# Sliding-window attention with sinks and a SwiGLU block: how the second group's keys and queries are loaded and transposed

## The chip, the cores and the metric

The kernel runs on one core of a Trainium2 chip. The metric is the device time of one execution in microseconds (us). TensorE multiplies matrices and transposes them against an identity, VectorE and ScalarE work elementwise and move results out of PSUM, GpSimd here mostly issues DMAs, and SyncE (SP) and ScalarE issue a few more.

## The reference

Cut to what matters: attention of 4 batches, 8 heads, 768 tokens, head width 64, where a query sees the 128 tokens up to its own and the first 4 tokens (the sinks); then a feed-forward block on the 3072 tokens.

```python
scores = scale * np.matmul(q, k.transpose(0, 1, 3, 2))
keep = is_sink | in_window              # first 4 keys, or 0 <= q - k < 128
a = softmax(np.where(keep, scores, -1e9))
x = np.matmul(a, v)                     # heads side by side: [3072, 512]
g = x @ w_gate                          # 512 -> 1536
out = ((g * sigmoid(g)) * (x @ w_val)) @ w_out
```

Inputs and output are float32 in DRAM; the kernel computes in bfloat16 and accumulates in float32.

## The kernel before

**Groups and blocks.** Attention goes by groups of 256 tokens, three to a batch, twelve in all (g = 0 to 11). The feed-forward block goes by blocks of tokens (SIZES, line 42: 256, 256, 256, 512, ...). The instruction order of every engine is written out by hand: `weave` runs over the feed-forward units (a gate unit is eight or four matmuls with `wg` and as many with `wv`, line 564; a down unit is twelve with `wo`, line 657) and puts attention steps of later groups between them. A program runs in that order on each engine; engines wait for each other, and for DMAs, by semaphores.

**Keys and queries.** The scores need keys and queries turned: head width on the partitions (two heads of 64 above each other), tokens along the row. The tiles `kT` and `qT` of a batch hold this for four pairs of heads. Four ways lead there:
- Group 0: `x0` and `st`, two tokens to a row, turned by `pair_T` (line 746).
- Group 1: `load_rows` (line 97) brings the tile `rows`, `step_T` (line 252) turns it. In `rows` a partition holds four successive tokens of one head (4 x 64 elements, 1 KB in DRAM, 512 B as bfloat16); partitions 0 to 63 belong to the even heads, 64 to 127 to the odd ones. Each 64x64 block is turned alone in a quarter of the array, 16 matmuls to a PSUM tile `pt` (two pairs of heads, all 256 tokens), and the copy out of PSUM puts the tokens back in order with a stride.
- Groups 2 and 3: `load_nat` (line 106) brings the tile `nat`, `step_TN` (line 273) turns it. In `nat` a partition is one token, with its eight heads side by side (each head's 64 elements are a piece of their own, 128 B as bfloat16). A 128x128 block (128 tokens, a pair of heads) is one transpose; four of them fill a bfloat16 PSUM tile `pn` (128 tokens, all heads).
- Groups 4 to 11: `nat` again, turned by DMA transposes on SP's queue.

All loads that convert float32 to bfloat16 are issued by GpSimd, in program order: `x0`, the keys and queries of group 1, the values of groups 0 and 1 (`va`, `load_v`, line 151), the first chunk of gate and value weights (`wg`, `wv`, `load_gate`, line 162); then, between a few small GpSimd computations (`kss`, `vsb`, for the sinks), two more weight chunks, the `nat` of group 2, and so on. `rows` and the `nat` of groups below 4 share a ring of three buffers (`rowp`) with the two `st` tiles.

**The work around the change on TensorE.** After group 0's scores come the transposes of group 1, then group 0's products with the values (line 494, tile `o`), the scores of group 1 (line 326, tile `s`) in three portions between them, the sink scores (line 432, `pk`), and the transposes of group 0's result (line 543, `px`), which give `xT`, the input of the first gate matmul (line 564, `pg`). The products of group 1 follow within the first gate units.

```python
    step_T(1, 0, 0, "a")
    step_T(1, 0, 1, "a")
    step_T(1, 1, 0, "v")
    step_T(1, 1, 1, "a")
    step_PV(0, 0, 0)
    step_PV(0, 0, 1)
    flush()
    step_S(1, 0)
```

`"a"` and `"v"` name the engine, ScalarE or VectorE, that copies the PSUM tile out.

Of the kernel before, what the change touches and what calls it, by code (L numbers as in the profile page):

```python
# [7 lines left out]
FP32 = mybir.dt.float32  # L8
BF16 = mybir.dt.bfloat16
# [5 lines left out]
def kernel(  # L15
# [12 lines left out]
    nc = tc.nc  # L28
    P = 128
    B, H, S, D = q.shape  # L30
# [8 lines left out]
    NP2 = H // 2  # L39
    GC = S // 256  # L40
# [14 lines left out]
    def pool(name, bufs, psum=False):  # L55
        if psum:
            return ctx.enter_context(
                tc.tile_pool(name=name, bufs=bufs, space=bass.MemoryType.PSUM))
        return ctx.enter_context(tc.tile_pool(name=name, bufs=bufs))
# [3 lines left out]
    rowp = pool("rowp", 3)  # L63
# [16 lines left out]
    def bank(shape, dtype, name):  # L80
        return psum.tile(shape, dtype, tag="b", name=name)


    rows, nats, vas = {}, {}, {}

    def by_rows(src, b, w, pairs, t0):

        hs = slice(2 * pairs.start + w, 2 * pairs.stop, 2)
        return src[b, hs, t0:t0 + 256].rearrange("p (m r) d -> m p (r d)", r=4)

    ALL = slice(0, NP2)

    def new_rows(g):
        rows[g] = rowp.tile([P, 2, NP2, 4 * D], BF16, tag="rows", name="rows")
        return rows[g]

    def load_rows(g, i):
        b, c = divmod(g, GC)
        if g not in rows:
            new_rows(g)  # L100
        for w in range(2):
            nc.gpsimd.dma_start(
                rows[g][64 * w:64 * (w + 1), i],
                by_rows((k, q)[i], b, w, ALL, c * 256))

    def load_nat(g):
        b, c = divmod(g, GC)
        x = (natp if g > 3 else rowp).tile(
            [P, 2, 2, DM], BF16, tag="nat" if g > 3 else "rows", name="nat")
        for i, src in ((0, k), (1, q)):  # L110
            for j in range(2):
                t0 = c * 256 + j * P
                nc.gpsimd.dma_start(  # L113
                    x[:, i, j].rearrange("p (h d) -> p h d", d=D),
                    src[b, :, t0:t0 + P].rearrange("h p d -> p h d"))
        nats[g] = x
# [26 lines left out]
    def load_v(g):  # L143
        if g in QG:
            return load_vm(g)
        b, c = divmod(g, GC)
        va = vpool.tile([P, 2, H, VS], BF16, tag=f"va{g}", name="va")
        nc.vector.memset(va[:, :, :, D:D + 1], 1.0)
        for j in range(2):
            t0 = c * 256 + j * P  # L150
            nc.gpsimd.dma_start(  # L151
                va[:, j, :, 0:D], v[b, :, t0:t0 + P].rearrange("h p d -> p h d"))
        vas[g] = va
# [19 lines left out]
    ident = const.tile([P, P], BF16)  # L173
# [41 lines left out]
    for i in range(2):  # L215
# [2 lines left out]
                   allow_small_or_imprecise_dtypes=True)  # L218
    nc.gpsimd.iota(tk, [[0, 1]], base=0, channel_multiplier=1,
                   allow_small_or_imprecise_dtypes=True)  # L220
    load_rows(1, 0)
    load_rows(1, 1)
    load_v(0)
    load_v(1)
    load_gate(0)
# [5 lines left out]
    kTs, qTs, es_t, e_t, xns, xTs = {}, {}, {}, {}, {}, {}  # L231
# [15 lines left out]
    def new_T(b):  # L247
        if b not in kTs:
            kTs[b] = kqtp.tile([P, NP2, S], BF16, tag="kT", name="kT")
            qTs[b] = kqtp.tile([P, NP2, S], BF16, tag="qT", name="qT")  # L250

    def step_T(g, i, p2, evict=None):
        b, c = divmod(g, GC)
        new_T(b)
        x = rows[g]
        pt = bank([P, 2, 256], FP32, "pt")
        for pp in range(2):
            p = 2 * p2 + pp
            for r in range(4):
                for w in range(2):  # L260
                    h = slice(64 * w, 64 * (w + 1))
                    nc.tensor.matmul(
                        pt[h, pp, 64 * r:64 * (r + 1)], x[h, i, p, r * D:(r + 1) * D],
                        ident[h, h], start=True, stop=True, skip_group_check=True)
        dst = (kTs, qTs)[i][b][:, 2 * p2:2 * p2 + 2, c * 256:(c + 1) * 256].rearrange(
            "q a (m r) -> q a m r", r=4)
        pt = pt.rearrange("q a (r m) -> q a m r", r=4)
        if (evict or ("a", "v")[i]) == "a":
            nc.scalar.copy(out=dst, in_=pt)
        else:  # L270
            nc.vector.tensor_copy(out=dst, in_=pt)

    def step_TN(g, i, j, evict="av"):

        b, c = divmod(g, GC)
        new_T(b)
        pt = bank([P, NP2, P], BF16, "pn")
        for p in range(NP2):
            nc.tensor.transpose(pt[:, p], nats[g][:, i, j, p * P:(p + 1) * P], ident)  # L279
        t0 = c * 256 + j * P  # L280
        dst = (kTs, qTs)[i][b][:, :, t0:t0 + P]
        if evict[i] == "a":
            nc.scalar.copy(out=dst, in_=pt)
        else:
            nc.vector.tensor_copy(out=dst, in_=pt)
# [531 lines left out]
    load_sinks(vcl, 1, B)  # L817
    build_maskq()

    step_T(1, 0, 0, "a")  # L820
    step_T(1, 0, 1, "a")
    step_T(1, 1, 0, "v")
    step_T(1, 1, 1, "a")
    step_PV(0, 0, 0)
    step_PV(0, 0, 1)
    flush()
# [98 lines left out]
```

## Time and profile before

| what | value |
|---|---|
| time, median of three runs | 233.85 us (233.03 to 235.38) |
| time of the profiled execution | 233.03 us |
| its span, first to last instruction | 231.2 us |
| TensorE matmuls, busy | 226.0 us, 98% of the span |
| VectorE, ScalarE, GpSimd, busy | 151.1, 106.3, 84.8 us |
| DMA packets | 112008, of which 99056 under 512 B |
| the transposes of group 1 (L262) | 64 matmuls, 9.45 to 11.09 us |
| first gate matmul (L564) starts | 15.09 us |

Times in the profile count from the start of the span. The 1.8 us between the span and the profiled execution's time lie around the span. "L262" is line 262; `pt<-ident,rows` is the tile written and the tiles read; "x64" is a number of instructions. PE is TensorE, PEld its weight loads, DVE VectorE, ACT ScalarE, POOL GpSimd, SP SyncE. An arrow in brackets names who ended an engine's idle time. A matmul's own length holds its way through the array, so matmuls that follow each other overlap in the listing; their pitch, start to start, is what a stream of them costs.

### The profile page before, as it was taken

Reading aid. Unit: us, or ns where it says so; the run is one execution under the profiler, and the core shown is the slowest. Engines: PE = TensorE matmul, PEld = TensorE weight load, DVE = VectorE, ACT = ScalarE, POOL = GpSimd, SP = SyncE. Lnnn points to the kernel's source line nnn. Section 1 sums busy time; section 2 is a strip of 40 time slices with the busy share of each in tenths; the row PEclk is TensorE's granted clock in tenths of the full one; section 3 lists DMA queues with packets and bytes.
Section 4 is the critical chain, followed back from the end, with each engine's and each line's share of the span. In section 5 each row is a group of like instructions: output and inputs, shape, how many; then the busy total and the mean of one; then the engine's idle time right before and its main releaser. Section 6 shows DMA issues by size and latency. Waiting matters only on the chain.

```text
span 231.2 us, 5467 instructions
## 1 busy us (share of the span) xinstructions
PE 226.0 (98%) x2171; PEld 126.8 (55%) x2171; DVE 151.1 (65%) x327; ACT 106.3 (46%) x212; POOL 84.8 (37%) x123
## 2 busy tenths in 40 slices
PE   7989999999999999999999999999999999999994
PEld 3669545786556854455454454454454544487443
DVE  5898888767650797960897960697960599778000
ACT  4784496367523827323626412735512823333221
POOL 8997965960500906904526064362000000000000
PEclk9999999999999999999999999999999999999999
DMA  7999999999998998998999999989814102000132
GB/s 134 164 188 178 179 199 206 163 155 125 154 168 211 80 132 103 145 197 124 134 124 118 147 87 203 144 107 131 94 48 136 48 0 45 3 0 0 69 116 91
DMA packets 112008, 28.04 MB, mean 121 GB/s; under 512 B 99056, under 2 KB 109040, under 8 KB 111984
## 3 DMA queue, kind: packets, MB, share of 16 engines
q0 software_dynamic: 79904, 14.29, 80.7%
q1 hardware_dynamic: 30672, 11.58, 28.5%
q10 hardware_dynamic: 1408, 1.84, 2.8%
q8 instruction: 17, 0.28, 0.5%
q14 instruction: 7, 0.06, 0.1%
HBM read 29.13 MB, written 6.29 MB: 153 GB/s over the span
## 4 chain that ended last, share of the span: by engine, by line
PE 93%; DMA 4%; DVE 1%; ACTq 0%; ACT 0%; issue 0%
PE pg L564 27%; PE pv L564 27%; PE pd L657 27%; PE o L494 3%; PE s L382 3%; DMA wg<-in_moe_w_gate_dram 3%; DMA st<-in_q_dram 2%; PE o L463 1%; PE pn L279 1%; PE o L454 1%; PE pk L432 1%; PE s L326 0%; PE px L543 0%; DVE kT L755 0%; PE pt L746 0%; PE s L765 0%
## 5 line engine op out<-in xcount | busy, mean ns | idle before, releaser
L592 DVE SCALAR_TENSOR_TENSOR u<-th,pg 128x512 bf16<-128x512 f32 x72 | 49.1, 683 | 45.3 <-ACT th L584 44.9
L564 PE MATMUL pg<-xT,wg 128*128 128x512 bf16 (+1 forms) x368 | 74.2, 333 | 0.5 <-DMA wg<-in_moe_w_gate_dram 0.5
L564 PE MATMUL pv<-xT,wv 128*128 128x512 bf16 (+1 forms) x368 | 74.1, 333 | 0.0
L584 ACT ACTIVATE th<-pg 128x512 f32<-128x512 f32 x72 | 43.8, 608 | 59.4 <-PE pg L564 59.2
L657 PE MATMUL pd<-wo,ht 128*128 128x512 bf16 (+2 forms) x300 | 65.9, 370 | 0.0
L564 PEld LDWEIGHTS <-wg 128*128 128x128 bf16 x368 | 35.2, 98 | 26.5 <-DMA wg<-in_moe_w_gate_dram 0.7
L564 PEld LDWEIGHTS <-wv 128*128 128x128 bf16 x368 | 34.6, 98 | 22.8 <-issue 0.2
L607 DVE TENSOR_TENSOR ht<-u,pv 128x512 bf16<-128x512 bf16 x60 | 41.2, 686 | 4.5 <-PE pv L564 0.4
L657 PEld LDWEIGHTS <-ht 128*128 128x128 bf16 x300 | 27.6, 98 | 28.4
L662 ACT ACTIVATE ot<-pd 128x512 f32<-128x512 f32 (+1 forms) x24 | 14.3, 595 | 50.2 <-PE pd L657 50.2
L395 ACT ACTIVATE e<-s 128x512 bf16<-128x512 f32 x54 | 28.5, 614 | 5.8 <-PE s L382 5.4
L113 POOL DMA_DIRECT2D nat<-in_k_dram x20 | 17.8, 896 | 28.6 <-DMA qT<-nat 27.1
L511 DVE TENSOR_TENSOR xn<-o,rcp 128x256 bf16<-128x256 f32 x45 | 17.9, 420 | 0.7
L128 POOL DMA_DIRECT2D vm<-in_v_dram x24 | 17.8, 772 | 1.1 <-DMA va<-in_v_dram 0.8
L113 POOL DMA_DIRECT2D nat<-in_q_dram x20 | 17.8, 908 | 1.0 <-DMA wg<-in_moe_w_gate_dram 0.8
L494 PEld LDWEIGHTS <-e 128*128 128x128 bf16 x256 | 11.5, 98 | 6.0 <-issue 0.2
L404 DVE TENSOR_TENSOR e<-e,maskq 128x768 bf16<-128x768 bf16 x24 | 13.1, 552 | 1.9 <-ACT e L395 1.9
L151 POOL DMA_DIRECT2D va<-in_v_dram x12 | 10.7, 921 | 4.5 <-DMA wo<-in_moe_w_out_dram 2.5
L703 POOL CAST warmed<-xT 1x1 f32<-1x1 bf16 x3 | 0.5, 175 | 28.5 <-DMA xT<-xn 28.5
L503 DVE RECIPROCAL rcp<-o 128x4 f32<-128x4 f32 x48 | 7.1, 171 | 4.8 <-PE o L494 4.5
L664 DVE TENSOR_SCALAR ot<-pd 128x128 f32<-128x128 f32 x1 | 0.3, 292 | 14.3 <-PE pd L657 14.3
L333 ACT ACTIVATE e<-s 128x512 bf16<-128x512 f32 x16 | 8.3, 625 | 0.3 <-PE s L326 0.3
(86 smaller groups left out, 141.4 us busy)
## 6 DMA issues: line engine op xcount, KB each, us to landing
out_dram<-ot SPq DMA_DIRECT2D x17, 256.0 KB
nat<-in_k_dram POOLq DMA_DIRECT2D x20, 128.0 KB, 4.2
nat<-in_q_dram POOLq DMA_DIRECT2D x20, 128.0 KB, 5.2
va<-in_v_dram POOLq DMA_DIRECT2D x12, 128.0 KB, 5.5
wg<-in_moe_w_gate_dram POOLq DMA_DIRECT2D x6, 256.0 KB, 7.1
wv<-in_moe_w_val_dram POOLq DMA_DIRECT2D x6, 256.0 KB, 7.6
wo<-in_moe_w_out_dram POOLq DMA_DIRECT2D x4, 384.0 KB, 11.1
out_dram<-ot ACTq DMA_DIRECT2D x6, 256.0 KB
```

What stands on the lines that cost most here:

```text
L113: nc.gpsimd.dma_start(x[:, i, j].rearrange("p (h d) -> p h d", d=D), src[b, :, t0:t0 + P].rearrange("h p d -> p h d"))
L128: nc.gpsimd.dma_start(vms[b][p0:p1, t - 1, :, 0:D], v[b, :, t0:t0 + p1 - p0].rearrange("h p d -> p h d"))
L395: nc.scalar.activation(e_t[g][:, e0:e0 + 512], pss[g][w, i], AF.Exp, scale=scale)
L404: nc.vector.tensor_tensor(e, e, m.broadcast_to([P, 2, 384]), op=ALU.mult)
L494: nc.tensor.matmul(o, l, r, start=(c == 0 and i == 0), stop=(i == len(mms) - 1), skip_group_check=True)
L511: nc.vector.tensor_tensor(xn, po[:, :, 0:D], rcp.broadcast_to([P, 4, D]), op=ALU.mult)
L564: nc.tensor.matmul(ps[:, i * n:(i + 1) * n], ws[fi][:, c, fo * P:(fo + 1) * P], xTs[tb][:, c], start=(c == 0), stop=(c == DMC - 1))
L584: nc.scalar.activation(th, pg, AF.Tanh, scale=0.5)
L592: nc.vector.scalar_tensor_tensor(u, th, 1.0, pg, op0=ALU.add, op1=ALU.mult)
L607: nc.vector.tensor_tensor(hts[tb][:, f:f + 512 // SIZES[tb]].rearrange("p a n -> p (a n)"), u, pv, op=ALU.mult)
L657: nc.tensor.matmul(po, hts[tb][:, f, ts * P:(ts + 1) * P], wos[f // n][:, f % n, lo:hi], start=(f == 0), stop=(f == DFC - 1))
L662: nc.scalar.activation(ot, po, AF.Copy, scale=0.5)
```

## The change

Group 1 takes the way of groups 2 and 3: `load_rows(1, 0)` and `load_rows(1, 1)` become `load_nat(1)` at the same place in GpSimd's order (again four DMAs of 128 KB each, as written), and the four calls of `step_T` become four calls of `step_TN` at the same place in TensorE's order. The copies out of PSUM stay on the same engines: ScalarE, ScalarE, VectorE, ScalarE. `load_rows`, `by_rows`, `new_rows` and `step_T` are removed. The ring `rowp` has the same tiles in the same order, one `nat` in place of one `rows`.

```diff
-    load_rows(1, 0)
-    load_rows(1, 1)
+    load_nat(1)
     load_v(0)
     load_v(1)
     load_gate(0)
...
-    step_T(1, 0, 0, "a")
-    step_T(1, 0, 1, "a")
-    step_T(1, 1, 0, "v")
-    step_T(1, 1, 1, "a")
+    step_TN(1, 0, 0, "aa")
+    step_TN(1, 0, 1, "aa")
+    step_TN(1, 1, 0, "av")
+    step_TN(1, 1, 1, "aa")
     step_PV(0, 0, 0)
```

The first argument after the group says keys (0) or queries (1). For `step_T` the next one is a half of the heads, for `step_TN` it is a half of the group's 256 tokens.

More of the change, by code (lines that the diff above doesn't have):

```diff
@@ L81, in bank @@
         return psum.tile(shape, dtype, tag="b", name=name)
[L84 to L104, printed above, removed]
+    nats, vas = {}, {}
     def load_nat(g):
@@ L250, in new_T @@
             qTs[b] = kqtp.tile([P, NP2, S], BF16, tag="qT", name="qT")
[L252 to L271, printed above, removed]
     def step_TN(g, i, j, evict="av"):
```

## Prediction

> **What bounds the kernel now.** I read the page first, for the engine that is always busy and for what ends its idle time.
>
> ```profile
> span 231.2 us, 5467 instructions
> PE 226.0 (98%) x2171; PEld 126.8 (55%) x2171; DVE 151.1 (65%) x327; ACT 106.3 (46%) x212; POOL 84.8 (37%) x123
> ...
> L564 PE MATMUL pg<-xT,wg 128*128 128x512 bf16 (+1 forms) x368 | 74.2, 333 | 0.5 <-DMA wg<-in_moe_w_gate_dram 0.5
> L564 PE MATMUL pv<-xT,wv 128*128 128x512 bf16 (+1 forms) x368 | 74.1, 333 | 0.0
> ```
>
> TensorE is busy for 226.0 of 231.2 us, and the feed-forward matmuls of L564 wait once in the whole run: 0.5 us, for the first gate weights. Second, TensorE's timeline around that wait and around the transposes that change:
>
> ```profile
> 9.45 1.64 PE L262 MATMUL pt<-ident,rows 64*64 64x64 bf16 x64
> 11.02 0.42 PE L494 MATMUL o<-va,e 128*128 128x65 bf16 x8
> 11.73 0.62 PE L326 MATMUL s<-qT,kT 64*128 64x128 bf16 x12 [0.29 <-DVE qT L271]
> 12.28 0.66 PE L494 MATMUL o<-va,e 128*128 128x65 bf16 x16
> ...
> 14.09 0.55 PE L326 MATMUL s<-qT,kT 64*128 64x128 bf16 x6
> 15.09 1.05 PE L564 MATMUL pg<-xT,wg 128*128 128x256 bf16 x8 [0.45 <-DMA wg<-in_moe_w_gate_dram]
> 16.07 0.29 PE L454 MATMUL o<-vsb,es 32*128 32x260 bf16 x4
> ...
> 24.75 0.61 PE L279 MATMUL pn<-ident,nat 128*128 128x128 bf16 x8
> ```
>
> TensorE is ready at 14.64 and starts the gate at 15.09, when the weights land. The chain of waits holds nothing but TensorE from there to the stores at the end. So the end is 15.09 plus a fixed run of matmuls: **what moves the first gate matmul moves the end one for one**, and what moves TensorE's readiness by less than 0.45 moves nothing. Third, what the weights wait for, in GpSimd's timeline, where all these loads are issued one behind the other:
>
> ```profile
> 3.23 1.28 POOL L102 DMA_DIRECT2D rows<-in_k_dram  x2
> 4.47 1.27 POOL L102 DMA_DIRECT2D rows<-in_q_dram  x2
> 5.67 3.60 POOL L151 DMA_DIRECT2D va<-in_v_dram  x4
> 9.17 0.85 POOL L162 DMA_DIRECT2D wg<-in_moe_w_gate_dram  x1
> ...
> 14.56 1.13 POOL L304 TENSOR_TENSOR vsb<-vcf,diag_h 128x260 bf16<-128x260 f32 x1
> 15.65 1.84 POOL L113 DMA_DIRECT2D nat<-in_k_dram  x2
> 17.46 1.78 POOL L113 DMA_DIRECT2D nat<-in_q_dram  x2
> ```
>
> GpSimd issues without a pause from 1.24 to 10.8, and the first wg (issued at 9.17, landed 5.87 later) stands behind the four loads that the change replaces. Fourth, the DMA view in two stretches of one microsecond, 10 to 11 (only va packets, of 128 B) and 16 to 17 (only weight packets, of 512 B):
>
> ```profile
> DMA packets 1196, 0.15 MB, mean 151 GB/s; under 512 B 1196, under 2 KB 1196, under 8 KB 1196
> ```
>
> ```profile
> DMA packets 398, 0.20 MB, mean 196 GB/s; under 512 B 16, under 2 KB 398, under 8 KB 398
> ```
>
> The same bytes take longer in short packets, and the engines work without a break from 6 us on, so extra service time is passed down the queue.
>
> **The change part by part.** *Loads.* Removed: four rows DMAs (64 partitions x 4 pairs = 256 packets of 512 B each, issued 0.61 apart: 3.23 to 5.67 is 2.44 for four). Added: four nat DMAs (128 partitions x 8 heads = 1024 packets of 128 B, the same bytes; the nat of group 2 is issued in the same form from 15.65 to 19.19, the va from 5.67 to 9.17, both 0.875 to 0.885 apart). Two prices follow.
> - By issue: 4 x (0.875 - 0.61) = 1.06 us later for everything behind it on GpSimd.
> - By service: 1024 packets at 1146 to 1196 in a microsecond are 0.86 to 0.89 us; 256 of 512 B take 0.67 at the 382 of that size seen in 16 to 17, and 0.77 at the 333 of the busier 7 to 8. Four times the difference is 0.35 to 0.9 us.
>
> Which of the two sets the landing? The va wait in a line today (first issued at 5.67, while their packets begin only near 8.8, as the rows end), so part of the later issue is taken up by that line, and service counts. But with 0.875 per issue and 0.88 per service the line hardly shrinks any more. I take **+0.75 for the landing of the first wg** (nearer to the service price), 0.35 to 1.06 as its ends: 15.05 becomes 15.8.
>
> *Transposes.* Removed: 64 quarter matmuls, 9.45 to 11.09. Added: 16 full ones. The 128-column matmuls of the first groups (pt of L746) follow each other by 0.106 us; the nat transposes of L279, later, by 0.056 (8 in 0.61, of which 0.22 is the last one's own length). TensorE runs at half rate until about 10.56 (below), so ten transposes go at 0.106 and the rest at 0.056: done at 10.9, if the data are there. The fourth load is issued at 3.23 + 3 x 0.875 = 5.86 and lands, at the 4.7 of the va, at 10.55; its four transposes then end at 10.95. Against 11.09: **nothing gained, nothing lost** on TensorE. That the instructions are four times fewer is worth nothing, because two quarters run at a time and a quarter has half the columns.
>
> *Evictions.* Four as before, three on ScalarE and one on VectorE. ScalarE's cost 0.53 each (L283, two in 1.07) for 0.54 (L269); VectorE's 0.42 (L285) for 0.70 (L271). But a tile now holds 128 tokens of all heads instead of all tokens of four heads, so the first scores of group 1 need all four evictions, where they needed one of each today. ScalarE is free of exponentials at 10.42, and three evictions end at 12.0: the scores start at 12.05 for 11.73, 0.3 later. The va that feed the products before and between land 0.75 later, 11.25 and 12.1 for the first two, and are used at 11.3 and 12.6: inside the same 0.3. TensorE and the copies of xT are then ready at 14.95 for 14.64. **The later wg (15.8) hides this**; without that cover, with wg at today's 15.05, 14.95 would still be in time.
>
> *What else is queued on GpSimd.* The sink keys (kss), the vsb product and the following weights and nat move with it. wv lands 16.45 today and is wanted at 16.79, the second wg 17.77 for 18.15, the k half of group 2 24.25 for 24.75: all are passed on by the same 0.75 as TensorE's own delay, so the margins of 0.3 to 0.5 stay. The thinnest is vsb: done at 15.69, wanted at 16.07; by issue it moves 1.06 and TensorE 0.75, which leaves 0.07. SP's and ScalarE's DMA queues are not touched: SP issues nothing from 5.2 to 40 us. From 57 us on GpSimd waits for what TensorE paces, and DMA has pauses.
>
> **Sum:** +0.75 for wg, 0 for transposes, 0 for evictions. Profiled execution: 233.03 + 0.75 = 233.8. That execution is the fastest of the three; on their median of 233.85 it is **234.6 us**, 0.3% slower, and inside the 1% that a measurement of this kernel can about tell from no change. Own range: +0.35 to +1.3 on the median (1.06 plus some vsb wait), 234.2 to 235.2.
>
> **The rivals.** *B, the clock steps up later.* The change sits on the very place where TensorE's rate doubles. The groups of TensorE before 10.4 and after 10.6:
>
> ```profile
> L262 PE MATMUL pt<-ident,rows 64*64 64x64 bf16 x36 | 1.2, 239 | 0.0
> ```
>
> ```profile
> L262 PE MATMUL pt<-ident,rows 64*64 64x64 bf16 x30 | 0.7, 201 | 0.0
> ```
>
> 239 ns becomes 192 to 201 ns inside this one group, and the pitch of 512 columns goes from 0.43 (the fill matmuls from 1.19 on) to 0.22 (256 columns in 0.109 at 15.09). So 1.1 us of quarter matmuls, 9.45 to 10.56, are the last work before the step. If transposes do not count as work for the clock, or wait for their data in that stretch, the step comes later, and each microsecond of matmuls until then costs half of one. Near end: the products that follow make up for it within 1.5 us, 0.7 us are lost and wg hides them: +0.75. Far end: as long again as from the first matmul (1.19) to the step, until 20: the 3.1 us of matmuls between 11 and 14.6 take 6.2, the gate starts at 18.05 (+2.96) and runs at half rate until 20 (+0.98): +3.9. I price it between, +2.5: 236.4. For it: the place, and the spread of the runs shown (233.0 to 235.4), which a step at a varying moment would give. Against it: the stretch stays filled with matmuls by the timing above, and no row shows that a transpose counts less.
> The Trainium skill has a rule for this: "TensorE: Matmul & The Clock Gate", Part 4, PE-mode transpose, says that transposes do not count as TensorE being busy in the way that matmuls do, and do not bring the full clock. By it the step is late and the sum is rival B's; no row here shows it either way, because the later nat and px transposes stand between matmuls.
>
> *C, a second margin breaks.* If the issue price holds (1.06) and short packets cost more beside the small loads of SP at the start, vsb, wv and group 2's k come after TensorE wants them, one stall each of 0.3 to 0.6: +1.06 and three times 0.45 give +2.4, 236.3. For: margins of 0.07 to 0.5. Against: landing and use shift together.
>
> *D, not slower.* The landing of wg does not move, because the line in front of the va takes up the whole later issue and the nat are served as fast as the rows (0.72 between rows landings, 0.83 between va landings, is little), while full-array work brings the clock's step sooner in those executions in which it comes late today; the median is 0.82 above the profiled run, and up to that much could go: 233.1, and more if an execution of 235.4 is the common case. Point of decision: wg lands by 15.3. Against: 1024 packets against 256, shown above.
>
> **How the numbers follow.** Forecast A 0.46 (0.42 within 1%, 0.04 above), B 0.30 (0.27 above), C 0.12 (0.09 above), D 0.12 (0.08 faster by over 1%, 0.04 within). Slower by over 1%: 0.04 + 0.27 + 0.09 = 0.40; faster 0.08; within 1% the rest, 0.52. The range starts at D's 233.1 and takes in B's far end, 233.85 + 3.9 = 237.8.
>
> **What would show it.** Right: nat issues 0.87 apart from 3.23, the first wg issued near 10.2 and landing near 15.8, one wait of TensorE before the gate of about 0.85, first scores of group 1 near 12.05, a gapless TensorE after that. B: 128-column transposes of group 1 all at 0.106 pitch and gate matmuls of 256 columns longer than 0.109. C: idle time of TensorE at L454 or L279. Wrong altogether: wg landing as today, or TensorE not ready by 15.8 at full clock.

## The result, and the profile after

| | before | after |
|---|---|---|
| median of 22 executions each | 233.33 us | 234.32 us |
| ratio, 95% interval | | 1.0037 (1.0022 to 1.0052) |
| profiled execution (time; span) | 233.03; 231.2 us | 233.87; 232.1 us |
| predicted | | 234.6 us, 233.1 to 237.8 |

The changed kernel is about 0.4% slower: the medians are 0.99 us apart, the two profiled executions 0.84. The page of after, whose line numbers are 42 lower than before (L564 is now L522):

```profile
span 232.1 us, 5368 instructions
PE 224.7 (97%) x2123; PEld 125.7 (54%) x2123; DVE 151.6 (65%) x327; ACT 106.6 (46%) x212; POOL 85.5 (37%) x123
...
q0 software_dynamic: 82976, 14.29, 82.1%
...
L522 PE MATMUL pg<-xT,wg 128*128 128x512 bf16 (+1 forms) x368 | 74.2, 333 | 1.0 <-DMA wg<-in_moe_w_gate_dram 1.0
L522 PE MATMUL pv<-xT,wv 128*128 128x512 bf16 (+1 forms) x368 | 74.2, 333 | 0.0
```

TensorE has 48 matmuls fewer and 1.3 us less busy time (its clock also stepped up earlier in this execution, at 5.43 for 10.56), and the span is 0.8 longer. GpSimd's queue moves the same 14.29 MB in 82976 packets where it was 79904. The one wait before the gate has grown from 0.5 to 1.0. TensorE's timeline of after:

```profile
8.61 0.62 PE L237 MATMUL pn<-ident,nat 128*128 128x128 bf16 x8
9.46 0.40 PE L237 MATMUL pn<-ident,nat 128*128 128x128 bf16 x4 [0.24 <-DMA nat<-in_q_dram]
10.32 0.40 PE L237 MATMUL pn<-ident,nat 128*128 128x128 bf16 x4 [0.46 <-DMA nat<-in_q_dram]
11.40 0.40 PE L452 MATMUL o<-va,e 128*128 128x65 bf16 x8 [0.68 <-ACT qT L241]
11.73 0.62 PE L284 MATMUL s<-qT,kT 64*128 64x128 bf16 x12
...
14.11 0.55 PE L284 MATMUL s<-qT,kT 64*128 64x128 bf16 x6
15.65 1.05 PE L522 MATMUL pg<-xT,wg 128*128 128x256 bf16 x8 [0.99 <-DMA wg<-in_moe_w_gate_dram]
16.62 0.29 PE L412 MATMUL o<-vsb,es 32*128 32x260 bf16 x4
16.85 0.66 PE L452 MATMUL o<-va,e 128*128 128x65 bf16 x16
17.55 1.05 PE L522 MATMUL pv<-xT,wv 128*128 128x256 bf16 x8
```

TensorE is ready at 14.66, as before (14.64). The gate starts at 15.65 for 15.09: +0.55. The first wv matmul starts at 17.55 for 16.79: +0.76, because wv landed at 17.50 (16.45 before). From there to the last store the feed-forward matmuls are 0.72 to 0.84 us late, with no further wait. And GpSimd's issues:

```profile
3.23 1.82 POOL L93 DMA_DIRECT2D nat<-in_k_dram  x2
5.02 1.79 POOL L93 DMA_DIRECT2D nat<-in_q_dram  x2
6.76 3.54 POOL L131 DMA_DIRECT2D va<-in_v_dram  x4
10.22 0.83 POOL L142 DMA_DIRECT2D wg<-in_moe_w_gate_dram  x1
```

wg is issued at 10.22 for 9.17: 1.05 later, where the prediction's price by issue was 1.06.

### The profile page after: what moved, and what is told of

Same layout as the page of the kernel before. It is cut to its first block, busy times and chain, and to the rows that moved or that the text cites. A ratio compares the mean times of both kernels' runs of the same rounds, so it can differ in the third digit from the quotient of the medians.

```text
span 232.1 us, 5368 instructions
## 1 busy us (share of the span) xinstructions
PE 224.7 (97%) x2123; PEld 125.7 (54%) x2123; DVE 151.6 (65%) x327; ACT 106.6 (46%) x212; POOL 85.5 (37%) x123
## 3 DMA queue, kind: packets, MB, share of 16 engines
q0 software_dynamic: 82976, 14.29, 82.1%
## 4 chain that ended last, share of the span: by engine, by line
PE 92%; DVE 3%; DMA 2%; POOL 1%; issue 1%; POOLq 0%
PE pg L522 27%; PE pv L522 27%; PE pd L615 27%; PE o L452 3%; PE s L340 3%; DMA wg<-in_moe_w_gate_dram 2%; PE o L421 1%; PE pn L237 1%; PE o L412 1%; POOL x L196 1%; PE pk L390 1%; DVE qT L713 0%; DVE x L694 0%; PE s L284 0%; DVE e L733 0%
## 5 line engine op out<-in xcount | busy, mean ns | idle before, releaser
L522 PE MATMUL pg<-xT,wg 128*128 128x512 bf16 (+1 forms) x368 | 74.2, 333 | 1.0 <-DMA wg<-in_moe_w_gate_dram 1.0
L522 PE MATMUL pv<-xT,wv 128*128 128x512 bf16 (+1 forms) x368 | 74.2, 333 | 0.0
L522 PEld LDWEIGHTS <-wg 128*128 128x128 bf16 x368 | 35.2, 98 | 27.0 <-DMA wg<-in_moe_w_gate_dram 1.2
L522 PEld LDWEIGHTS <-wv 128*128 128x128 bf16 x368 | 34.6, 98 | 22.9 <-DMA wv<-in_moe_w_val_dram 0.2
L93 POOL DMA_DIRECT2D nat<-in_k_dram x22 | 19.6, 898 | 29.7 <-DMA qT<-nat 20.2
L93 POOL DMA_DIRECT2D nat<-in_q_dram x22 | 19.6, 906 | 1.6 <-DMA wv<-in_moe_w_val_dram 0.9
```

The source lines that it names most:

```text
L93: nc.gpsimd.dma_start(x[:, i, j].rearrange("p (h d) -> p h d", d=D), src[b, :, t0:t0 + P].rearrange("h p d -> p h d"))
L522: nc.tensor.matmul(ps[:, i * n:(i + 1) * n], ws[fi][:, c, fo * P:(fo + 1) * P], xTs[tb][:, c], start=(c == 0), stop=(c == DMC - 1))
```

## The experiments

The theory: the changed loads hold up the first weights, by GpSimd's longer issue and by the longer service of short packets, and nothing else counts. The rivals: the transposes, the copies or the clock behind them; and, within the theory, issue against service. Ratios are against the kernel before on the same chip.

**The loads without the transposes.**

```diff
-    step_TN(1, 0, 0, "aa")      # and three more: 16 full transposes
+    step_TQ(1, 0, "aa")         # 64 quarter matmuls on nat
+    step_TQ(1, 1, "va")
...
+    nc.tensor.matmul(pts[t][64 * w:64 * (w + 1), p, j],
+        nats[g][h, i, j, (2 * p + w) * D:(2 * p + w + 1) * D], ident[h, h], ...)
```

> The changed kernel with its loads (four nat DMAs of 1024 packets), but group 1 turned by 64 quarter matmuls again, which fill two PSUM banks for keys and two for queries, one per half of a token block. If the loads decide: the first wg lands near 15.6 and the end stays at 0.7 to 1.0 us above the kernel before. If the full transposes or the step of the clock behind them decide: the end goes back to the kernel before, 0 to +0.3.

Median 234.44 us, ratio 1.0059 (1.0034 to 1.0083): the whole loss with none of the full transposes. Its profiled execution is the longest of the twelve, with half clock for 6.8 us; in it TensorE waits for queries and values and not for wg:

```profile
PE o L473 <- DMA va<-in_v_dram: 1.4, 2, 0.8
...
PE pt L240 <- DMA nat<-in_q_dram: 1.2, 2, 0.6
```

The four executions at full clock (a mean granted clock of 0.997 or more) have a median of 234.23, 1.1 above the 17 such of the kernel before on that chip (233.09). The transposes are not the cause. The copies still need all four tiles here, so this run does not part them from the loads; the next two, with the copies as before, do.

**The short packets without the layout by tokens.**

```diff
-        return src[b, hs, t0:t0 + 256].rearrange("p (m r) d -> m p (r d)", r=4)
+        return src[b, hs, t0:t0 + 256].rearrange("p (m r) d -> m r p d", r=4)
...
-        rows[g] = rowp.tile([P, 2, NP2, 4 * D], BF16, tag="rows", name="rows")
+        rows[g] = rowp.tile([P, 2, 4, NP2, D], BF16, tag="rows", name="rows")
```

> The kernel before, with rows loaded in another order inside the partition so that each piece is one head of one token: four DMAs of the same bytes to the same 64 partitions, 1024 packets of 128 B for 256 of 512 B; the 64 quarter matmuls and the copies are as before. If the number of packets decides: issues 0.87 apart for 0.61, first gate matmul near 15.6, end +0.7 to +0.9 against the kernel before. If the layout by tokens, the transposes or the clock decide: 0.

Median 234.63 us, ratio 1.0064 (1.0041 to 1.0087). The number of packets alone brings the loss, and a little more than expected. Its issues are only 0.80 to 0.85 apart (wg at 9.98), but the packets are served more slowly than those of va in the kernel before (151 GB/s); the DMA view from 9 to 10 us:

```profile
DMA packets 1081, 0.14 MB, mean 137 GB/s; under 512 B 1081, under 2 KB 1081, under 8 KB 1081
```

These pieces lie on 64 partitions and nat's on 128; whether that makes the slower service was not tried. TensorE itself was late here as well: one of VectorE's mask operations (L780) took 1.47 us where it took 0.33 before, TensorE waited 1.55 us for the conversion behind it, and at the gate it waited for wg only 0.33. How much of the loss beyond the expected one comes from either is open.

**Issue without packets.**

```diff
     load_rows(1, 1)
+    for _ in range(4):
+        nc.gpsimd.memset(pause, 1.0)
     load_v(0)
```

> The kernel before with four GpSimd memsets of a scratch tile (128x195, 0.28 us each by the row of the one at L815) between the rows loads and the values: everything behind is issued 1.1 us later, and no packet is added. If issue alone sets the landing: wg lands 1.1 later, end +1.1. If service sets it and the line in front of the values takes up the rest (their packets begin 3.1 after the issue, those of the first x loads 2.5): wg +0.5, end +0.5. If the DMA engines were so far behind that issue does not count: 0.

Median 235.64 us over 8 executions, ratio 1.0074 (1.0043 to 1.0106). GpSimd's timeline shows that the memsets took 1.24, and what follows is late by that:

```profile
5.67 1.29 POOL L225 MEMSET pause<- 128x195 f32 x4
6.91 3.55 POOL L151 DMA_DIRECT2D va<-in_v_dram  x4
10.41 0.80 POOL L162 DMA_DIRECT2D wg<-in_moe_w_gate_dram  x1
```

wg landed at 16.13, 1.08 later, with not a packet more. One landing against one is weak evidence: a second execution of the kernel before has wg at 16.07 (below). But the two executions of this run at full clock, 233.99 and 234.17, are 0.9 and 1.1 above 233.09, and the count of packets told with the next run agrees. So issue alone moves the weights almost in full. The line in front of the values took up little, where half of the delay was expected to vanish: "service" as the only price falls. The end is later than +1.1 in most executions; why is told at the clock, below. The profiled one is of these: TensorE waits 1.0 and 0.5 us for va, then has half clock, and does not wait for wg.

**Issue earlier.** The opposite: two DMAs taken off the head of GpSimd's queue.

```diff
+    for h0 in (4, 6):
+        for i in range(2):
+            nc.sync.dma_start(st[i][:, h0:h0 + 2], by_two((k, q)[i], h0, 2))
-    for i in range(2):
-        nc.gpsimd.dma_start(x0[:, i, 4:8], by_two((k, q)[i], 4))
...
     pair_T(1)
+    for p in (2, 3):
+        cast(0, p)
+        cast(1, p)
```

> The changed kernel with the last half of group 0's keys and queries taken off GpSimd: SP loads them as float32 in the same way as the first half, and VectorE and ScalarE convert them (two more casts of 0.3 to 0.45 us each). The bytes still pass the same 16 DMA engines, but GpSimd issues two DMAs fewer (1.66 us) ahead of everything else. If issue sets the landing of the weights: the first wg is issued near 8.7 and lands near 14.1, the wv near 16; no wait before the gate, and the end at the kernel before or up to 0.4 below it. If service sets it: wg still near 15.6, end as in the changed kernel, +0.8 to +1.0.

> The same edit on the kernel before: GpSimd's two x loads go to SP, rows and quarter matmuls stay. If issue sets the landing: wg lands near 13.5, the gate starts when TensorE is ready (14.6), end -0.4 against the kernel before; the changed kernel's own edit would then cost less than 0.3 on top (x8 against x7), since TensorE's readiness, and no landing, is the bound. If service sets it: 0.

x8: 236.28 us, ratio 1.0099 (1.0063 to 1.0135); x7: 238.24 us, 1.0195 (1.0153 to 1.0236). Both miss: the end says nothing on issue, since group 0's data came late by SP's queue. In x8 ScalarE waits 1.5 and 1.7 us for these loads before its two added casts (0.4 us each), VectorE 1.7, and TensorE for the casts (x8, waits of TensorE):

```profile
PE pt L705 <- ACT x L697: 2.1, 2, 1.1
```

The weights do say something. In x8 wg is issued at 8.61, 1.61 earlier than in the changed kernel, and takes 6.8 us to land (15.44) where it took 5.4 (15.60):

```profile
8.61 0.78 POOL L142 DMA_DIRECT2D wg<-in_moe_w_gate_dram  x1
```

```profile
DMA to landing us min/median/max: 6.8/6.8/6.8
```

(the first line is GpSimd's timeline, the second the view of the tile wg for that one issue).

Landings scatter by about 1 us between executions of one program (below). Steadier is the moment by which as many 512 B packets have ended, behind those of rows, as wg has (512 of them), counted over the packets of the trace: 13.88 and 13.73 in two executions of the kernel before, 14.74 and 14.79 in two of the changed kernel. In x3 it is 14.92, about 1.1 later for 1.24 of later issue. In x8 it is 14.59 and in x7 13.90: about 0.2 earlier than in the changed kernel and 0.1 later than in the kernel before, though wg is issued 1.61 and 1.70 earlier.

So a later issue delays the weights nearly in full, and an earlier one hardly hastens them: this fits issue and service taking about equally long, the longer of the two counting. It is not shown cleanly, since in x7 and x8 SP's float32 loads pass the DMA engines in the same time.

**One deadline or two.**

```diff
-    load_v(1)
-    load_gate(0)
+    load_gate(0, (0,))
+    load_v(1)
+    load_gate(0, (1,))
```

> The changed kernel with the first gate weights issued ahead of the values of group 1, 1.75 us earlier; the first value weights stay behind them. If the landing of wg alone sets the end: no wait before the gate, which starts at 14.7, and the end is 0.8 to 1.0 us earlier than in the changed kernel. If the first wv is a second deadline behind it (wanted 1.7 after the gate's start, landed at 17.5 in the changed kernel): the gate starts at 14.7, TensorE waits about 1.0 us for wv instead, and the end is where the changed kernel has it.

Median 234.33 us, ratio 1.0033 (1.0016 to 1.0051): with wg out of the way (landed at 14.07) the end does not move (the changed kernel: 234.32), at full clock neither (nine executions, 234.38). So there is a second deadline. In the profiled execution, which had a stretch of half clock, the gate waits for VectorE's xT alone, and then the first wv matmul for wv:

```profile
16.09 1.03 PE L523 MATMUL pg<-xT,wg 128*128 128x256 bf16 x8 [0.19 <-DVE xT L509]
...
18.10 1.05 PE L523 MATMUL pv<-xT,wv 128*128 128x256 bf16 x8 [0.16 <-DMA wv<-in_moe_w_val_dram]
```

**Both deadlines eased.** Half of group 1's values goes behind wg and wv, and the one product that needs it into the second gate unit.

```diff
-    load_v(1)
+    load_v(1, (0,))
     load_gate(0)
+    load_v(1, (1,))
...
         a = gate_a(tb, f)               # gate_held
         step_PV(1, 0, 0)
-        step_PV(1, 1, 0)
...
+        step_PV(1, 1, 0)                # gate_first
         step_PV(1, 0, 1, "a")
```

> The changed kernel with the second half of group 1's values (one DMA, 0.87 us of issue) moved behind the first wg and wv, and the product that needs it moved from the first gate unit to the second. If the first wg and wv are the deadlines that the change misses: both land 0.87 earlier, and the end comes down by 0.7 to 0.9 us from the changed kernel, near the kernel before. If TensorE's own order or its clock in the first 16 us made the loss: no gain.

Median 234.06 us, ratio 1.0014 (0.999 to 1.0037). wg landed at 14.95, wv at 16.34, both 0.65 or more earlier than in the changed kernel, as meant; but only 0.3 to 0.4 us of the expected 0.7 to 0.9 came back. In the profiled execution TensorE itself was late: it waits for nat and va while group 1 is turned, falls to half clock (12.45 to 15.87) and starts the gate at 15.99 without waiting for wg. That is not the whole reason: the eight executions at full clock, 233.96, are still 0.75 above those of the kernel before on that chip. A third deadline stands behind the two. The second chunk's wg is issued at 12.49, as in the changed kernel (12.48), and landed at 18.57 for 18.81; the matmuls that need it start at 18.92 there. By these two profiles about 0.3 is all that the edit could bring.

The same edit on the kernel before, as the version that might beat both:

> The kernel before with the second half of group 1's values behind the first wg and wv, and its product moved to the second gate unit (the edit that took 0.3 to 0.4 off the changed kernel). If the landing of the first weights bounds the kernel before as well: wg at 14.2 for 15.05, the gate starts when TensorE is ready, end -0.3 to -0.5. If TensorE's readiness, with its clock, bounds it as often: 0 to -0.2.

> The kernel before with half of group 1's values behind the first weights, once more beside the kernel before on another occasion: if its 0.33 us were more than chance, the median is again 0.2 to 0.5 below and the interval moves off 1; if not, within 0.1.

233.02 against 233.35 us (ratio 0.999, 0.9964 to 1.0015) and, the second time, 232.99 against 233.16 (0.9979, 0.9956 to 1.0001). Lower both times, by less than was expected, and neither interval leaves 1: not shown to be faster. wg landed at 14.80 and at 14.38, where 14.2 was expected, and in the first of the two profiles TensorE does wait at the third deadline, the second wg:

```profile
18.37 0.83 PE L566 MATMUL pg<-xT,wg 128*128 128x256 bf16 x6 [0.30 <-DMA wg<-in_moe_w_gate_dram]
```

**The changed kernel again.**

> The changed kernel once more, beside the kernel before on one chip, for its granted clock execution by execution: where the clock is granted throughout, +1.0 us against such executions of the kernel before if issue sets the landing (1.05), +0.5 if service does; where one window of half clock (mean 0.993) falls into the start, less than that, because the wait for the weights covers a part of it.

Median 234.46 us, ratio 1.0044 (1.0018 to 1.007). Its profile has the same issues as the first one to 0.01 us, but wg landed at 16.92 instead of 15.60:

```profile
16.97 1.05 PE L522 MATMUL pg<-xT,wg 128*128 128x256 bf16 x8 [2.51 <-DMA wg<-in_moe_w_gate_dram]
```

All executions of the two kernels whose clock is on record, by the mean granted clock (half clock for 3.4 us is 0.993 of a span of 231):

| | before: executions, median | after: executions, median |
|---|---|---|
| clock granted throughout (0.997 and more) | 69, 233.16 us | 16, 234.22 us |
| about one stretch at half clock (0.99 to 0.997) | 24, 234.05 us | 17, 234.40 us |
| less | 1, 234.06 us | 1, 235.00 us |

The record of the clock begins at its first step up: the profile of before has a mean of 1.000, though its first 10.56 us ran at half rate. So the rows do not say when that step came. At full clock the change costs 1.06 us, the size of the price by issue; resampling both rows gives 0.8 to 1.4, which does not part it from the upper end of the price by service. The change also goes with more frequent stretches of half clock (25 of 94 before, 18 of 34 after; 4 of 24 and 7 of 12 on the chip where both ran side by side), but such a stretch costs 0.9 before and 0.2 after. This fits TensorE having slack of its own now, in the wait for the weights.

**Fewer instructions, and where an instruction packet falls.** Another thing had moved. In the DMA view from 14.5 to 15.5 us of after stands a row that was at 11.8 before:

```profile
q8 instruction: 1, 0.02, 5.9%
```

It is the first of 16 packets of 16 KB (17 before), about one for each 256 instructions of TensorE, weight loads included. With 96 instructions fewer it falls among the packets of wg and wv.

```diff
-            for r in range(4):
-                for w in range(2):
...
-                        pt[h, pp, 64 * r:64 * (r + 1)], x[h, i, p, r * D:(r + 1) * D],
-                        ident[h, h], start=True, stop=True, skip_group_check=True)
+            for w in range(2):
...
+                    pt[h, pp], x[h, i, p, 0:D], zero[h, 0:256],
```

> The kernel before, loads and evictions untouched, with 16 quarter matmuls of 256 columns in place of 64 of 64 columns: the same time on the array, 48 matmuls and 48 weight loads fewer. (Group 1's keys and queries are zeros here: the moving operand is a tile of zeros.) In the kernel before, the first 16 KB instruction packet of the DMA view comes after 271 instructions of TensorE, at 11.8 us, on the packets of the values; in the changed kernel after 277, at 14.75, on those of the first weights. If that move is a part of the loss: the packet comes near 14.7 here too, wg or wv lands up to 0.9 later, end +0.2 to +0.6. If the loads alone make the loss: end within 0.2 of the kernel before, wherever the packet falls.

> The kernel before in one more profile, to see how far landings and the step of the clock differ between executions of one program: wg within 0.5 of 15.05 and the instruction packet again after some 271 instructions, if these are fixed by the program; the step of the clock anywhere between 5 and 13 us.

y1 leaves out the turning itself (group 1's keys and queries are zeros). 233.41 against 233.35 us, ratio 0.9995 (0.9975 to 1.0014). The packet came at 15.47, and in the profiled execution TensorE did wait for wv:

```profile
PE pv L563 <- DMA wv<-in_moe_w_val_dram: 0.9, 1, 0.9
```

But that execution took 234.65, the longest of its twelve; the median has not moved. The kernel before, looked at again (233.99 us), has the packet at 12.51 and its own late landing, wg at 16.07 for 15.05:

```profile
PE pg L564 <- DMA wg<-in_moe_w_gate_dram: 1.5, 1, 1.5
```

So single executions differ by a microsecond in this landing, with the packet early or late, and its place is no part of the 1 us between the medians.

## Why the prediction was right

It forecast 0.3% slower, by later weights and by nothing else, and 0.4% was measured. That the forecast time, 234.6 us, is so near the measured 234.32 is partly luck: it started from 233.85, the median of three runs, 0.52 above the later median of 22, and added 0.75 where 0.99 was measured. Step by step:

- **What bounds the kernel**: right. From the first gate matmuls on, the delay is passed to the end nearly unchanged (0.72 to 0.84 us); x3, at full clock, says the same without the edit.
- **Price by issue, +1.06**: 1.05 in the profile. **Price by service, 0.35 to 0.9**: not measured alone. By the count of packets told above, the size of wg is through 0.86 later in the first pair of profiles and 1.06 in the second, wv behind it 0.95 and 1.15; these delays hold both prices.
- **The choice of +0.75 between them** is the mis-sized term, as far as the runs can tell. It rested on the line in front of the values taking up part of the later issue. x3 shows that it takes up little (1.24 of later issue, about 1.1 in the packets), and x7 and x8 fit the longer price counting, which is issue. The medians at full clock give 1.06 (0.8 to 1.4). Over all executions it is 0.99, with an interval of 0.5 to 1.2 that still holds 0.75. The profiled pair alone (+0.55 for wg, +0.76 for the end) would have looked like the chosen value; single landings scatter more than the two prices differ.
- **Transposes, 0**: right. x1 has the loss with 64 quarter matmuls.
- **Copies, +0.3 hidden**: TensorE was ready at 14.66, not 14.95. ScalarE was free at 9.7 instead of 10.4, in an execution whose clock stepped up at 5.4; the scores began at 11.73, as before. What the 0.3 would cost without cover was not seen.
- **"The margins stay"**: not the one of wv. wg had its landing moved by 0.55 and wv by 1.05, so the 0.34 between wv's landing and its use was spent and 0.2 us were added to the end. That is rival C's mechanism at a place that the prediction had called safe; x4 and x6 show it as a second and a third deadline behind the first.
- **Rival B, the clock**: the cost is small, but the clock is involved. The feared mechanism, transposes that hold back the step up, is not what the profiles show: in after the clock is full from 5.43 us on, through all 16 transposes. What does happen in half of the executions is a fall after an early step. x4, in the windows view (PEclk is the column after the engines; the two behind it are DMA):

```profile
6.00:12.00 6.00, 3.90 (x61) 2.43 (x59) 4.70 (x17) 4.83 (x11) 5.96 (x8) 1.00 2.09 143
12.00:15.40 3.40, 3.40 (x50) 2.40 (x46) 2.02 (x9) 3.05 (x7) 3.32 (x7) 0.50 1.90 168
15.50:18.00 2.50, 2.25 (x35) 1.58 (x34) 2.50 (x6) 1.75 (x4) 2.46 (x4) 1.00 1.45 196
```

  TensorE is busy for 3.9 of the 6 us in which it waits for nat and va, and then has half its clock for 3.4 us. x1 has the same fall for 6.8 us with quarter matmuls in place of transposes (8 of its 12 executions are below 0.997), and x3 too (6 of 8) with the old loads issued late. The common element is the waiting: from 5.5 to 12.0 us TensorE is busy for 4.1 to 4.6 us in the four profiles that fall at 12 us (x1, x3, x4, x6), and for 4.7 to 5.2 in the six whose clock also steps up by 6.1 and does not fall (before_again, both of after, both of x5, y1). That the idle time brings the fall is inferred from this; it was not tried by filling the gaps.
  The Trainium skill ("TensorE: Matmul & The Clock Gate", Part 1) puts the clock's window at about 3.4 us and says that an idle window brings the half clock back. The lengths here, 3.4 and 6.8, agree, though TensorE was partly busy in the stretch ahead. The Trainium skill says on the same page (Part 4) that transposes do not count as busy in the way that matmuls do. As the cause of the fall this is not needed here: x1, which turns group 1 by quarter matmuls, falls as often.
- **Rival D, not slower**: fell with wg's later landing.

## What to carry to other kernels

A load's price has two rates, the issuing engine's and the DMA engines'. Work out both for everything queued behind it; here the longer one came nearer than a value between them. Four times fewer instructions on TensorE bought almost nothing: at full clock the 64 quarters follow each other by 0.016 us (before_again) and the 16 transposes by 0.057, about 1.0 us against 0.9, and TensorE waits for the weights behind them anyway. And when a first deadline is lifted, check the next ones before counting the gain: wg ahead of its place changed nothing, because wv came next, and with both moved the second wg came next.

## What the runs showed of the hardware

The same load, issued at the same time by the same program, landed 1.0 to 1.3 us apart in two executions (wg at 15.05 and 16.07 before, 15.60 and 16.92 after). The bulk of the packets was steadier: as many as wg has were through within 0.15 us of each other (13.88 and 13.73, 14.74 and 14.79), and the landing came 0.9 to 2.3 us behind that. Which of the last packets made the difference was not told apart. A wait that one profile shows for a DMA has at least the uncertainty of the landing, and a difference of half a microsecond needs medians, not a pair of profiles. The moment of the clock's first step differs as widely between executions of one program (10.56 and 4.25 us before, 5.43 and 4.99 after).
